# The second matrix product of a fused convolution and MLP kernel: 26 products of 4-row blocks in place of 5-row blocks, fewer VectorE taps, some sums as accumulating DMAs

## The chip, the cores and the metric

The kernel runs on one core of one Trainium2 chip. The metric is the device time of one execution in microseconds. Before the change it is 2314.07 us, the median of three runs (2314.03 to 2314.65).

## The reference

The input x has 8 sequences of 4096 tokens with 192 channels, in 32-bit floats. Eight heads of 24 channels each get a causal depthwise convolution of 7 taps, whose weights are a softmax over the taps. The result goes through a two-layer MLP with 2048 hidden units.

```python
w = softmax(weight, axis=-1)                  # (8 heads, 7 taps), 1e-9 in the divisor
out[b, s, h, g] = sum_k w[h, k] * x_pad[b, s + k, h, g]    # x padded by 6 zeros ahead
x = out.reshape(32768, 192)
h = x @ moe_w_in                              # (192, 2048)
g = h * (1 / (1 + exp(-1.702 * h)))
return g @ moe_w_out                          # (2048, 192), float32
```

The two weight matrices arrive as 64-bit values and are rounded on the chip.

## The kernel before

**Tiling.** The 32768 tokens are worked off in 32 steps, called `big`: 4 pairs of sequences times 8 chunks of 512 tokens, two chunks (one of each sequence) at a time. Step 0 is done apart (`first_step`, `second_first`), beside the rounding of the weights and the making of their sums; this first stage ends about 95 us into the run. Steps 1 to 31 are one loop. Tokens lie along the free axis, 256 (`T`) to a half, and channels and hidden units along the partitions.

**First product.** `hidden(big, v, ...)` runs twice a step, for v = 0 and v = 1, each for half of the hidden units. It is a product scheme with fewer multiplications than the plain one: 21 terms each, a list `TERMS` of sums of weights by sums of convolution blocks, and each term is a pair of two 64x512 matmuls on the two row halves of TensorE (L577). Terms gather in PSUM banks (`x`, `y`, `z`, `sums`), ScalarE copies some of them to SBUF (k15, k16, k18, k19, k20 in the tile `room`, L607), VectorE adds (L611) and ScalarE applies the Gelu with the sigmoid into the tile `g` (L598, L600).

**Second product.** `second(...)` makes out = g·w_out by a scheme of products of blocks: `g` has 16 rows of 128 hidden units, cut into 3 blocks of 5 rows and 1 row over. Sums of the blocks of `g` (VectorE, 128x1280, L649 to L693 in the second `hidden` and L893 to L930 in `second`) multiply forms, that is sums of blocks of w_out, made once in the first stage. A round is three matmuls of 128x256 on three column groups and a fourth, of a side product, on the column group left over (L867); there are 81 rounds. When a side product ends, ScalarE copies it out of PSUM (L881, 32x256), main products are copied by ScalarE (96x256) and joined by VectorE (L908 to L972), turned by VectorE (L819) and stored by DMA.

**The convolution for a later step.** While step big runs, step big + 2 is prepared. The channels are three blocks of 64. Each of two of them (c = 1, 2) is made by VectorE: seven instructions, one multiplication (L492) and six multiply-adds (L494). Block c = 0 is made by ScalarE, which multiplies (L501), and GpSimd, which adds (L505). GpSimd also makes the sums of convolution blocks (`sums_c`, L388 and L390). The blocks are then copied to the other half of the partitions by DMAs that SyncE issues (`cross`).

**What sets the order.** Every engine runs its instructions in the order of the program, which is written by hand: the scheduler is off (`manual_schedule`), and the framework adds the semaphores. VectorE's convolution work is a list (`todo`), taken from by `work(us)` at chosen places, as many items as the given number of microseconds holds by the costs noted beside them. The taps are another list (`ready`), taken from by `next_tap`: in `second`, one at every fourth round from 54 on (`LATE, EVERY = 54, 4`), and then all of the six additions that follow:

```python
for k in (*range(1, K), 0):
    yield "", 1.0, lambda k=k: tap_times(big, k)
for k in range(1, K):
    yield "", 0.0, lambda k=k: add_tap(big, k)
```

`need(label)` takes a list up to a label, `give` lets the copies of a step's blocks go, and `cross_when` holds them back until then.

Of the kernel before, what the change touches and what calls it, by code (L numbers as in the profile page):

```python
# [15 lines left out]
def kernel(  # L16
# [99 lines left out]
    NS, ND = 3, 5  # L116
    assert len(PAIRS) * 4 == NF == NS * ND + 1
    g = consts.tile([P, 2, NF, TOK], F32)


    ROW = {1: 2, 2: 0, 3: 1}
    COL = {1: (0, 0), 2: (0, 1), 3: (1, 1), 4: (1, 0)}

    def block(r, j):

        n, o = COL[j]
        i = ND * ROW[r]
        return g[:, n, i : i + ND, o * T : (o + 1) * T]

    def rest(j):  # L130
        n, o = COL[j]
        return g[:, n, NF - 1 :, o * T : (o + 1) * T]


# [6 lines left out]

    BLK = ND * T
    t_s = osbs[:, 0:BLK].rearrange("p (k t) -> p k t", k=ND)
    spare = consts.tile([P, 3, T], F32)
    t_a, t_8 = (
        flat_room[:, i * BLK : (i + 1) * BLK].rearrange("p (k t) -> p k t", k=ND) for i in range(2)
    )

    def kept(i):

        return flat_room[0 : NC * Q, 2 * BLK + i * T : 2 * BLK + (i + 1) * T]

    e0, e1, e2 = (spare[0 : NC * Q, i, :] for i in range(3))
    e3 = block(3, 3)[0 : NC * Q, 0, :]


# [59 lines left out]
    FORMS = 12  # L218
    F1, F3, F5, N7, F8, N9, F11, F13, N14, F15, F16, F19 = range(FORMS)
    w_form = consts.tile([P, FORMS, ND, HD], F32)  # L220

    def w_part(m, r):
        i = ND * ROW[r]
        return w_out_s[:, m - 1, i : i + ND, :]

    def form(i):
        return w_form[:, i, :, :]

    BEGIN_O = [
        (F1, (1, 1), 1), (F5, (1, 2), 1), (N14, (2, 1), 1), (F16, (1, 2), 1), (F13, (1, 2), -1),  # L230
        (F19, (2, 2), 1), (F15, (1, 1), 1), (F11, (1, 3), 1), (F3, (2, 3), 1),
    ]
    ADD_O = [(F1, (2, 1)), (F5, (1, 3)), (N14, (2, 3)), (F16, (2, 2)), (F13, N14), (F19, N14), (F15, F5)]
    BEGIN_2 = [(N9, F1, 1), (F8, F5, 1), (N7, F5, -1)]
    ADD_2 = [(N9, (2, 3)), (F8, (2, 2)), (N7, (2, 1)), (F11, N9), (F3, F8)]
    TURN_O = [(N14, N14, -1), (N9, N9, -1)]

# [6 lines left out]
    assert PIECE == CW * D and 3 * PIECE <= NB * T and 3 * PIECE <= 2 * NJ * XW and 3 * PIECE <= FORMS * ND * HD  # L244
    places = w_in_s[:, 4 * NC : NA, :].rearrange("p a f -> p (a f)")
    b12, b22 = (g[:, 1, i:, :].rearrange("p i t -> p (i t)") for i in (6, 2))
# [180 lines left out]
    def of_form(j):  # L427
        return w_part(*j) if isinstance(j, tuple) else form(j)

    def begin_forms(items):  # L430
        for dst, src, sign in items:
            if sign == 1:
                act.copy(form(dst), of_form(src))
            else:
                act.mul(form(dst), of_form(src), -1.0)

    def add_forms(items):
        for dst, src in items:
            nc.gpsimd.dma_start(out=form(dst), in_=of_form(src), accum_op=ALU.add)
# [35 lines left out]

    taps = [block(1, 3)[:, 0:2, :], block(1, 3)[:, 2:4, :], block(3, 1)[:, 3:5, :]]
    taps += [block(1, 4)[:, 0:2, :], block(1, 4)[:, 2:4, :], block(3, 3)[:, 3:5, :]]
    assert len(taps) == K - 1
    first_taps = [g[:, 0, k, :].rearrange("p (n t) -> p n t", n=2) for k in (2, 3, 6, 7, 10, 11)]

    def tap_home(big, k):
        return (first_taps if big < 3 else taps)[k - 1]
# [15 lines left out]
    def tap_times(big, k):  # L498

        dst = tap_home(big, k) if k else own(big)[:, 0:2, :]  # L500
        act.mul(dst, conv_src(big, 0, k), cw[:, 0, k : k + 1])  # L501

    def add_tap(big, k):
        dst = own(big)[:, 0:2, :]
        nc.gpsimd.tensor_add(dst, dst, tap_home(big, k))  # L505
# [22 lines left out]
    given = {True: 0, False: -1}  # L528

    def cross_when(early, *what):  # L530
        if given[early] < what[0] - 1:
            waiting[early].append(what)
        else:
            cross(*what)

    def give(early, big):
        given[early] = big
        for what in waiting[early]:
            cross(*what)
        waiting[early].clear()  # L540

    def prepare(big):
# [9 lines left out]
        yield from convs(2, 0) if big == 1 else convs(2, 1)  # L552
# [40 lines left out]
    def gelu(b, u, v, src):  # L593
        m, n = divmod(b, 2)
        i = 2 * (v * len(PAIRS) + PAIRS.index((m, u)))
        if isinstance(src, list):
            for h in range(2):
                act.activation(g[:, n, i + h, :], src[h], AF.Gelu_apprx_sigmoid)  # L598
        else:
            act.activation(g[:, n, i : i + 2, :], src, AF.Gelu_apprx_sigmoid)  # L600
# [17 lines left out]
    def hidden(big, v, x, z, y, sums, work, fetch, last=lambda: None):  # L618
# [5 lines left out]


# [3 lines left out]
        pe(sums, 12)  # L629
        copy2(k15, sums)  # L630
        pe(x, 5, 17)
# [3 lines left out]
        pe(sums, 0)  # L635
        copy2(k16, sums)
        last()
# [5 lines left out]
        if v or big == 1:  # L643
            work(3.2 if v else 1.6)
# [3 lines left out]
        if v:  # L648
            vec.tensor_add(t_s, block(2, 1), block(2, 4))  # L649
            vec.tensor_sub(block(2, 1), block(2, 1), block(3, 1))  # L650
        work(2.6 if v else 1.2)
# [3 lines left out]
        copy2(k18, x)  # L655
        pe(z, 11)
# [6 lines left out]
        work(1.1)  # L663
        gelu(B22, 1, v, k19)
        gelu(B22, 0, v, k15)
        pe(y, 8)
        pe(sums, 1, 9, first=True)
        pe(y, 15)
        if v and big == 1:
            turn_next()  # L670
        else:
            work(2.2 if big > 1 and not v else 1.1)
# [5 lines left out]
        if v:  # L678
            vec.tensor_sub(t_a, block(2, 3), block(3, 3))
# [5 lines left out]
        work(1.2)  # L685
# [3 lines left out]
        work(0.7)  # L689
        sum2(vec.tensor_add, k18, k18, sums)  # L690
        if v:
            vec.tensor_add(block(2, 3), block(2, 2), block(2, 3))
            vec.tensor_sub(t_8, t_s, block(3, 1))  # L693
# [5 lines left out]
    def second_first(fetch):  # L699
# [9 lines left out]

        ws = [w_out_s[:, m, :, :] for m in range(2)]  # L710
        gs = [g[:, n, :, :] for n in range(2)]
        a11, a12, a21, a22 = (four(t, pi) for t in ws for pi in first)
        b11, b12, b21, b22 = (four(t, pi) for pi in first for t in gs)
        t1, t2 = (place4(flat_room[:, i * nk * TOK : (i + 1) * nk * TOK]) for i in range(2))
        flat_spare = spare.rearrange("p i t -> p (i t)")
        w4 = nk * HD
        s1, s2 = (place4(flat_spare[:, i * w4 : (i + 1) * w4]) for i in range(2))
# [11 lines left out]
        def listed(w, t):  # L729
            return [(w[:, v, h, :], t[:, v, h, :]) for v in range(2) for h in range(2)]  # L730

        def plainly(m, n):
            return [p for pi in other for p in listed(four(ws[m], pi), four(gs[n], pi))]
# [35 lines left out]
        begin_forms(BEGIN_O)  # L769
        add_forms(ADD_O)  # L770
# [12 lines left out]
        begin_forms(BEGIN_2)  # L783
        add_forms(ADD_2)
# [47 lines left out]
    LATE, EVERY = 54, 4  # L832

    def second(big, bx, by, bs, vec_work, final, last):
# [4 lines left out]
        (m1, sa), (m2, m3), (sb, sc) = bx, bs, by  # L839
        s16, s21, s22, s2, s23, s12, v8, s14, s17, q13 = (kept(i) for i in range(10))  # L840
        s13, s4, s11 = (block(3, 1)[0:n3, i, :] for i in range(3))
        sc12, s1v, s24, u5 = e0, e1, e2, e3

        side, rounds_done = [], [0]

        def side_product(w, t, to, first=True, banks=(sa, sb, sc)):

            for c, bank in enumerate(banks):
                dst = bank[n3:, 0:T]
                for k in range(t.shape[1]):  # L850
                    last = k == t.shape[1] - 1
                    side.append((dst, w[:, k, chunk_cols(c)], t[:, k, :], first and k == 0, last and chunk(to, c)))

        one = lambda m: w_out_s[:, m - 1, NF - 1 :, :]
        side_product(w_part(2, 2), block(2, 4), s12)
        side_product(form(F16), block(2, 2), s16)
        if not last:
            side_product(one(2), rest(2), s22, first=False)
        side_product(form(F16), block(2, 1), s17)
        side_product(one(1), rest(1), s11, first=False)  # L860
        side_product(form(F1), block(1, 1), s1v)
        side_product(form(F1), block(1, 2), s4)
        if last:
            side_product(one(2), rest(2), s22, banks=(m3, m2, sb))
# [4 lines left out]
        def go(bank, h, w, t, first=True, left=None):  # L869

            dst = bank[0:n3, h * T : (h + 1) * T]
            steps = [(w[:, k, :], t[:, k, :]) for k in range(ND)]
            if left:
                steps.append((w_out_s[:, left[0] - 1, NF - 1, :], rest(left[1])[:, 0, :]))
            for k, (wk, tk) in enumerate(steps):
# [7 lines left out]
                if rounds_done[0] >= LATE and rounds_done[0] % EVERY == LATE % EVERY:  # L883
                    next_tap()
# [334 lines left out]
```

## Time and profile before

| | |
|---|---|
| median of three runs | 2314.07 us (2314.03 to 2314.65) |
| span of the profiled execution | 2312.2 us |
| that execution's own time | about 1.9 us over its span, by the median |
| TensorE busy | 2304.8 us, 100% |
| VectorE, ScalarE, GpSimd busy | 2005.1, 1376.9, 432.4 us |
| granted clock | 1.000 |
| DMA | 137.99 MB, mean 60 GB/s |

The span runs from the first instruction to the last. Busy times are those of instructions on the engine; the share is of the span. TensorE is named PE, its weight loads PEld, VectorE DVE, ScalarE ACT, GpSimd POOL and SyncE SP. A group of the profile is a line of the program, an engine, an operation, output and inputs by the program's names, shapes and a count; then the busy time of all and the mean duration of one in ns, then the idle time of the engine ahead of them and what ended most of it.

### The profile page before, as it was taken

What the parts mean: (1) busy time and instruction counts of PE and PEld (TensorE: products, weight loads), DVE (VectorE), ACT (ScalarE), POOL (GpSimd) and SP (SyncE); (2) the same over time, 40 slices, a digit from 0 to 9 for tenths busy, and PEclk for the clock granted to TensorE, in tenths of its full rate; (3) what the DMA queues carried; (4) which work ended last, traced back from release to release, by engine and by line L of the source; (5) the groups of instructions that cost most, each with busy time, mean ns of one, the idle gap of its engine ahead of it and who ended that gap; (6) DMA issues with size and microseconds to landing.
All of it is one profiled execution on the core that took longest, in us unless ns stands there. A gap on an engine that the chain in (4) does not pass through costs nothing.

```text
span 2312.2 us, 60320 instructions
## 1 busy us (share of the span) xinstructions
PE 2304.8 (100%) x25982; PEld 1217.8 (53%) x25982; DVE 2005.1 (87%) x2819; ACT 1376.9 (60%) x2554; POOL 432.4 (19%) x451
## 2 busy tenths in 40 slices
PE   9999999999999999999999999999999999999999
PEld 5355555555555555555555555555555555555556
DVE  8898889888898888898888988889888898888877
ACT  7555665566655556555566555665565655556644
POOL 0311222102221022211122211222102221022200
PEclk9999999999999999999999999999999999999999
DMA  8632322223221233112331132321223321231010
GB/s 185 121 67 60 70 52 47 56 57 70 65 48 43 57 70 70 42 43 58 70 70 43 44 69 57 70 53 45 57 57 70 68 45 43 57 70 45 17 43 16
DMA packets 199899, 137.99 MB, mean 60 GB/s; under 512 B 109008, under 2 KB 190544, under 8 KB 195664
## 3 DMA queue, kind: packets, MB, share of 16 engines
q1 hardware_dynamic: 197072, 130.98, 25.7%
q0 software_dynamic: 1728, 2.95, 0.8%
q8 instruction: 204, 3.34, 0.6%
q14 instruction: 63, 0.52, 0.1%
q10 hardware_dynamic: 832, 0.20, 0.0%
HBM read 53.15 MB, written 25.17 MB: 34 GB/s over the span
## 4 chain that ended last, share of the span: by engine, by line
PE 99%; ACT 0%; DVE 0%; DMA 0%; issue 0%; SPq 0%; DVEq 0%; ACTq 0%
PE slot L577 35%; PE slot L867 33%; PE sums L577 16%; PE sums L867 14%; PE slot L746 2%; DMA xin<-in_x_dram 0%; ACT conv_t L1029 0%; DVE xt L471 0%; DVE conv_t L494 0%; SPq L99 0%; ACT conv_t L354 0%; ACT conv_t L353 0%; DVE osbs L819 0%; ACT conv_t L523 0%; ACT conv_t L1025 0%
## 5 line engine op out<-in xcount | busy, mean ns | idle before, releaser
L577 PE MATMUL slot<-conv_t,w_in_s 64*128 64x512 f32 x3740 | 852.5, 590 | 0.3 <-DVE w_in_s L373 0.3
L867 PE MATMUL slot<-g,w_form 128*32 128x256 f32 x6700 | 772.5, 379 | 0.0
L577 PEld LDWEIGHTS slot<-conv_t,w_in_s 64*128 64x128 f32 x3740 | 369.0, 187 | 432.1 <-issue 386.9
L505 POOL TENSOR_TENSOR conv_t<-conv_t,g 128x512 f32<-128x512 f32 x180 | 244.8, 1360 | 1448.6 <-ACT conv_t L501 1436.8
L867 PEld LDWEIGHTS slot<-g,w_form 128*32 128x32 f32 x6700 | 399.6, 110 | 134.9 <-ACT g L598 23.5
L867 PE MATMUL sums<-g,w_form 128*32 128x256 f32 x3530 | 461.8, 379 | 0.0
L867 PE MATMUL slot<-g,w_out_s 128*32 128x256 f32 x4432 | 442.0, 379 | 0.0
L577 PE MATMUL sums<-conv_t,w_in_s 64*128 64x512 f32 x1660 | 405.4, 591 | 0.3 <-DVE w_in_s L373 0.3
L600 ACT ACTIVATE g<-room 128x1024 f32<-128x1024 f32 x310 | 324.5, 1073 | 90.9 <-DVE room L611 90.9
L494 DVE SCALAR_TENSOR_TENSOR conv_t<-xt,cw,conv_t 128x512 f32<-128x512 f32 (+1 forms) x390 | 309.3, 793 | 10.1 <-ACT conv_t L492 3.2
L867 PEld LDWEIGHTS slot<-g,w_out_s 128*32 128x32 f32 x4432 | 226.0, 110 | 97.5
L867 PEld LDWEIGHTS sums<-g,w_form 128*32 128x32 f32 x3530 | 233.3, 110 | 65.6
L607 ACT COPY room<-slot 128x512 f32<-128x512 f32 x434 | 231.5, 602 | 57.3 <-PE slot L577 57.3
L577 PEld LDWEIGHTS sums<-conv_t,w_in_s 64*128 64x128 f32 x1660 | 165.7, 187 | 189.1 <-issue 154.1
L598 ACT ACTIVATE g<-slot 128x512 f32<-128x512 f32 x334 | 179.7, 590 | 88.8 <-PE slot L577 88.8
L881 ACT COPY room<-slot 32x256 f32<-32x256 f32 x245 | 89.8, 367 | 205.8 <-PE slot L867 200.2
L867 PE MATMUL sums<-g,w_out_s 128*32 128x256 f32 x1706 | 205.3, 379 | 0.0
L867 PE MATMUL slot<-room,w_form 128*32 128x256 f32 x2340 | 182.1, 379 | 0.0
L611 DVE TENSOR_TENSOR room<-slot,room 128x512 f32<-128x512 f32 x248 | 156.1, 680 | 20.4 <-ACT room L607 20.4
L611 DVE TENSOR_TENSOR room<-room,sums 128x512 f32<-128x512 f32 x124 | 79.1, 679 | 70.2 <-PE sums L577 70.2
L611 DVE TENSOR_TENSOR room<-room,slot 128x512 f32<-128x512 f32 x124 | 79.1, 678 | 64.5 <-PE slot L577 64.5
L607 ACT COPY room<-sums 128x512 f32<-128x512 f32 x186 | 100.0, 591 | 58.8 <-PE sums L577 58.8
(212 smaller groups left out, 2665.5 us busy)
## 6 DMA issues: line engine op xcount, KB each, us to landing
xin<-in_x_dram SPq DMA_DIRECT2D x240, 180.0 KB, 4.1
conv_t<-conv_t SPq DMA_DIRECT2D x62, 512.0 KB, 6.2
out_dram<-osbs SPq DMA_DIRECT2D x186, 128.0 KB, 2.6
conv_t<-conv_t SPq DMA_DIRECT2D x62, 256.0 KB, 3.1
conv_t<-conv_t SPq DMA_DIRECT2D x62, 64.0 KB, 4.5
xin<-in_x_dram SPq DMA_DIRECT2D x16, 160.0 KB, 3.3
w_form<-w_out_s POOLq DMA_DIRECT2D x7, 240.0 KB, 4.1
osbs<-in_moe_w_out_dram SPq DMA_DIRECT2D x2, 768.0 KB, 8.3
```

The source lines that it names most:

```text
L494: vec.scalar_tensor_tensor(out=dst, in0=src, scalar=tap, in1=dst, op0=ALU.mult, op1=ALU.add)
L505: nc.gpsimd.tensor_add(dst, dst, tap_home(big, k))
L577: nc.tensor.matmul(slot[h], w_in_s[halves[h], a, v * P : (v + 1) * P], src, start=first, stop=True, skip_group_check=True,)
L598: act.activation(g[:, n, i + h, :], src[h], AF.Gelu_apprx_sigmoid)
L600: act.activation(g[:, n, i : i + 2, :], src, AF.Gelu_apprx_sigmoid)
L607: act.copy(bank(dst, h), bank(src, h))
L611: op(*(bank(t, h) for t in (dst, a, b)))
L746: nc.tensor.matmul(chunk(bank, c), w[:, chunk_cols(c)], t, start=first and i == 0, stop=not more and i == len(steps) - 1, skip_group_check ...
L867: nc.tensor.matmul(dst, w, t, start=first, stop=last, skip_group_check=True)
L881: act.copy(to, d)
```

## The change

- `second` becomes 26 products of blocks of 4 rows (4 blocks, no row over). There are 78 rounds, in the order of a list `PLAN` of items (main, side, go, sum, acc, seed, join, turn, store, tap, cross, final).
- `g` is laid out anew, as `[P, 4, 2, 2, 4, 256]`, and the Gelus write into it with a stride.
- There are 28 sums of blocks of g in a step: 22 on VectorE with 128x1024 (five in the second `hidden`, `EARLY_G`, seventeen in `PLAN`) and six as accumulating DMAs that GpSimd issues, of 512 KB each (one in `EARLY_G`).
- "Seeds" are copies, some negated, by ScalarE of a PSUM or SBUF value into PSUM or SBUF, ahead of a product that adds to it or of a join.
- Convolution block c = 2 leaves VectorE and becomes taps like c = 0, so there are 14 taps a step: seven in `PLAN`, from round 50 to 72, and seven in `hidden` with v = 0 (`taps_at`). Each tap now issues its multiplication and, but for the first of a block, GpSimd's addition right behind it.
- The copies to the other half of the partitions go in pieces of at most three blocks, at the `cross` items in `PLAN`.
- In `hidden` with v = 1 the calls of `work` go (but for step 1), and with v = 0 the first terms are in another order.
- The forms of w_out are made by 19 additions on GpSimd (128x384) and 6 negations on ScalarE, in place of copies on ScalarE and 12 accumulating DMAs.

```diff
-    NS, ND = 3, 5
+    NG = 4
...
-    g = consts.tile([P, 2, NF, TOK], F32)
+    g = consts.tile([P, NG, 2, 2, NG, T], F32)
...
+    SUMS_O = [
+        (8, 7, "+", 6), (9, 5, "+", 7), (10, 2, "+", 6), (11, 3, "-", 5), (12, 3, "-", 6), (13, 3, "+", 7),
...
-    def tap_times(big, k):
-
-        dst = tap_home(big, k) if k else own(big)[:, 0:2, :]
-        act.mul(dst, conv_src(big, 0, k), cw[:, 0, k : k + 1])
-
-    def add_tap(big, k):
-        dst = own(big)[:, 0:2, :]
-        nc.gpsimd.tensor_add(dst, dst, tap_home(big, k))
+    def tap(big, c, k):
+
+        dst = own(big)[:, 2 * c : 2 * c + 2, :]
+        home = tap_home(big, c, k) if k else dst
+        act.mul(home, conv_src(big, c, k), cw[:, c, k : k + 1])
+        if k:
+            nc.gpsimd.tensor_add(dst, dst, home)
...
+    def cross_now(early, big, b0, b1):
+        if early or big == 1:
+            cross(big, b0, b1)
+        else:
+            pieces.extend((big, b, min(b + 3, b1)) for b in range(b0, b1, 3))
...
-        yield from convs(2, 0) if big == 1 else convs(2, 1)
+        yield from convs(2, 0) if big == 1 else convs(1)
...
-        for k in (*range(1, K), 0):
-            yield "", 1.0, lambda k=k: tap_times(big, k)
-        for k in range(1, K):
-            yield "", 0.0, lambda k=k: add_tap(big, k)
+        for c in (0, 2):
+            for k in range(K):
+                yield "", 1.0, lambda c=c, k=k: tap(big, c, k)
...
+        else:
+            pe(x, 5)
+            pe(sums, 12)
+            copy2(k15, sums)
+            pe(x, 17)
+            taps_at(1)
         gelu(B11, 0, v, x)
         if not v:
             pe(z, 7, first=True)
         pe(sums, 0)
+        taps_at(1)
         copy2(k16, sums)
+        taps_at(2)
         last()
...
-        work(2.6 if v else 1.2)
+        early(1)
+        if not v or big == 1:
+            work(1.2)
         pe(sums, 13)
         copy2(k19, sums)
         pe(x, 2)
         copy2(k18, x)
+        taps_at(2)
...
+    EARLY_G = [
+        [(6, 6, "-", 10)], [(1, 7, "-", 6), (1, 1, "-", 11)], [(0, 5, "+", 6), (8, 0, "acc")],
+        [(2, 9, "-", 0)],
+    ]
+    PLAN = [
...
+        ("tap",), ("go", 2), ("main", 21, 7, "p2", 0), ("go", 1), ("sum", 6, 14, "+", 6), ("go", 1), ("tap",),
+        ("side", 7, 20, "k1"), ("go", 2), ("sum", 6, 6, "-", 17), ("main", 10, 14, "p0", 0), ("go", 2),
+        ("tap",), ("seed", "k5", "p2", 1), ("cross",), ("join", "k10", "k10", "+", "k8"), ("go", 2),
+        ("join", "p2", "p4", "+", "k3"), ("main", 8, 8, "p1", 0, 0, 2), ("go", 1),
+        ("join", "k8", "k9", "+", "k5"), ("tap",), ("go", 1), ("join", "k8", "k7", "-", "k8"),
+        ("main", 4, 6, "p4", 0), ("go", 1), ("turn", 1, 0, 1, "k10"), ("go", 1),
+        ("join", "k3", "p1", "+", "k6"), ("go", 1), ("tap",), ("join", "k3", "p0", "-", "k3"), ("go", 1),
+        ("join", "k6", "k0", "-", "p0"), ("side", 8, 5, "k0"), ("main", 15, 12, "p2", 0), ("go", 2),
+        ("join", "k7", "k4", "-", "p4"), ("go", 1), ("tap",), ("join", "k7", "k7", "+", "k3"), ("go", 1),
+        ("join", "k2", "k2", "-", "k1"), ("main", 12, 18, "p3", 0), ("go", 1), ("turn", 0, 0, 0, "k7"),
+        ("go", 1), ("join", "k6", "k6", "+", "p4"), ("tap",), ("go", 1), ("turn", 1, 1, 1, "k2"), ("go", 1),
+        ("turn", 1, 0, 0, "k6"), ("store", 0, 0), ("main", 24, 19, "p5", 0), ("go", 2), ("final",),
...
+    ]
+
+    def sum_g(dst, a, op, b=None):
+
+        if op == "acc":
+            nc.gpsimd.dma_start(out=spot(dst), in_=spot(a), accum_op=ALU.add)
+        else:
+            add_up(spot, dst, a, op, b)
...
+        for item in PLAN:
+            ops[item[0]](*item[1:])
...
-        second(big, x, y, sums, work, lambda: copy2(sums, z) if more else None, not more)
+        second(big, x, y, sums, lambda: copy2(sums, z) if more else None, not more)
```

In `PLAN`, "go n" issues n rounds, "main f s to" starts the product of form f by block or sum s into the PSUM half-bank to (p0 to p5, two to a bank), "side" does the same for the fourth column group, and "join", "seed", "turn" name half-banks or SBUF values of 96x256 (k0 to k11). Spots 0 to 4 of the sums are scratch, those from 5 on are the sixteen blocks of `g` itself.

More of the change, by code (lines that the diff above doesn't have):

```diff
@@ L474, in transpose_x, with tap_home @@
         )
[L476 to L482, printed above, removed]
+    taps = [spot(i)[:, k : k + 2, :] for i in TAP_SPOTS for k in (0, 2)]
+    first_taps = [row(0, k) for k in (2, 3, 6, 7)]
+    def tap_home(big, c, k):
+        return (first_taps if big < 3 and c == 0 else taps)[(3 * c + k - 1) % len(taps)]
     def conv_src(big, c, k, ns=slice(0, 2)):
@@ L677, in hidden @@
         gelu(B21, 1, v, x)
[L678 to L679 removed]
+        early(3)
         fetch()
@@ new lines, with second, value, product @@
+    SIDE_HALF = (0, 0, 1, 0, 1, 0, 1)
+    def second(big, bx, by, bs, final, last):
+        n3 = NC * Q
+        mains, sides = (bs[0], bx[0], by[0]), (bx[1], bs[1], by[1])
+        side, count = [], [0]
+        now = {}
+        stored = {0: 0, 1: 0}
+        def value(name):
+            i = int(name[1:])
+            return mains[i // 2][0:n3, i % 2 * T : (i % 2 + 1) * T] if name[0] == "p" else kept(i)
+        def product(f, s, k0=0, k1=NG):
+            return [(form(FORM_OF[f])[:, k, :], spot(s)[:, k, :]) for k in range(k0, k1)]
@@ L866, in one_matmul, with begin_side @@
         def one_matmul(dst, w, t, first, last):
             nc.tensor.matmul(dst, w, t, start=first, stop=last, skip_group_check=True)
[L869 to L875, printed above, removed]
+        def begin_side(f, s, to, *ks):
+            steps = product(f, s, *ks)
+            for c in range(NC):
+                turns, i = divmod(count[0], NC)
+                h = SIDE_HALF[turns]
+                count[0] += 1
+                dst = sides[i][n3:, h * T : (h + 1) * T]
+                for k, (w, t) in enumerate(steps):
+                    end = k == len(steps) - 1
+                    side.append((dst, w[:, chunk_cols(c)], t, k == 0 and h == 0, end and chunk(value(to), c)))
@@ L972, in second, with seed, out_turn @@
-        add(s22, s22, q13 if last else s4)
-        done(2, 2, s22)
-        if last:
-            store(big, 0, 1, (nc.scalar, nc.sync, nc.scalar))
-        else:
-            store(big, 0)
-        assert not side
+        def seed(dst, src, sign):
+            if sign == 1:
+                act.copy(value(dst), value(src))
+            else:
+                act.mul(value(dst), value(src), -1.0)
+        def out_turn(m, n, o, src):
+            turn(m, n, blocks(value(src)), slice(o * T // Q, (o + 1) * T // Q))
@@ new lines, in out_store @@
+        def out_store(n, o):
+            if last:
+                queues = (nc.sync, nc.scalar) if o else (nc.scalar, nc.sync)
+                store(big, n, o, queues + queues[0:1])
+                return
+            stored[n] += 1
+            if stored[n] == 2:
+                store(big, n)
+        ops = dict(
+            sum=sum_g, acc=lambda d, a: sum_g(d, a, "acc"), main=begin_main, side=begin_side, go=go, seed=seed,
+            join=lambda d, a, op, b: add_up(value, d, a, op, b), turn=out_turn, store=out_store,
+            tap=next_tap, cross=cross_piece, final=final,
+        )
@@ L980 @@
+        for item in PLAN:
+            ops[item[0]](*item[1:])
+        assert not side and not now["steps"] and count[0] == NC * len(SIDE_HALF)
+        while pieces:
+            cross_piece()
     todo, ready = [], []
```

279 lines of the change are left out of this document (93 added, 186 removed), and 24 rows, old and new, of tables (PLAN, SUMS_O).

## The prediction

> **What bounds the kernel now.** First the totals of the page, its clock row and the chain of waits:
>
> ```profile
> PE 2304.8 (100%) x25982; PEld 1217.8 (53%) x25982; DVE 2005.1 (87%) x2819; ACT 1376.9 (60%) x2554; POOL 432.4 (19%) x451
> ...
> PEclk9999999999999999999999999999999999999999
> ...
> PE 99%; ACT 0%; DVE 0%; DMA 0%; issue 0%; SPq 0%; DVEq 0%; ACTq 0%
> PE slot L577 35%; PE slot L867 33%; PE sums L577 16%; PE sums L867 14%; PE slot L746 2%; DMA xin<-in_x_dram 0%; ACT conv_t L1029 0%; DVE xt L471 0%; DVE conv_t L494 0%; SPq L99 0%; ACT conv_t L354 0%; ACT conv_t L353 0%; DVE osbs L819 0%; ACT conv_t L523 0%; ACT conv_t L1025 0%
> ```
>
> The reader is to see that TensorE never stops: whatever the others do is hidden, and the clock never falls. So a round less is worth its full time, and any wait that appears is paid in full. Then the timeline of TensorE: one second product (L867) begins at 1059.48 and the next first product (L577) at 1094.58, so 81 rounds take 35.10 us, **0.4333 us each**; a big step is 36.25 + 35.10 us. The groups by shape price what moves:
>
> ```profile
> L494 DVE SCALAR_TENSOR_TENSOR conv_t<-xt,cw,conv_t 128x512 f32<-128x512 f32 x378 | 303.5, 803 | 9.9 <-ACT conv_t L492 3.2
> L505 POOL TENSOR_TENSOR conv_t<-conv_t,g 128x512 f32<-128x512 f32 x180 | 244.8, 1360 | 1448.6 <-ACT conv_t L501 1436.8
> L501 ACT ACTIVATE g<-xt,cw 128x512 f32<-128x512 f32 x180 | 126.5, 719 | 2.3
> ...
> L881 ACT COPY room<-slot 32x256 f32<-32x256 f32 x245 | 89.8, 367 | 205.8 <-PE slot L867 200.2
> ...
> L893 DVE TENSOR_TENSOR g<-g 128x1280 f32<-128x1280 f32 x31 | 46.0, 1484 | 0.0
> ...
> L959 DVE TENSOR_TENSOR room<-room 96x256 f32<-96x256 f32 x30 | 38.9, 1297 | 0.0
> L972 DVE TENSOR_TENSOR room<-room,g 96x256 f32<-96x256 f32 x30 | 29.6, 987 | 0.0
> L966 DVE TENSOR_TENSOR spare<-spare,g 96x256 f32<-96x256 f32 x30 | 28.3, 944 | 3.5 <-DVE spare L964 0.5
> L911 DVE TENSOR_TENSOR room<-room 96x256 f32<-96x256 f32 x31 | 12.9, 415 | 0.0
> L964 DVE TENSOR_TENSOR spare<-spare,slot 96x256 f32<-96x256 f32 x31 | 12.6, 406 | 0.7 <-PE slot L867 0.7
> ```
>
> L959, L966 and L972 are joins of the same shape as L911, yet two to three times as long. The timelines of GpSimd and VectorE at the end of one second product say why:
>
> ```profile
> 1093.75 8.53 POOL L505 TENSOR_TENSOR conv_t<-conv_t,g 128x512 f32<-128x512 f32 x6 [49.47 <-ACT conv_t L501]
> ```
>
> ```profile
> 1093.98 1.33 DVE L959 TENSOR_TENSOR room<-room 96x256 f32<-96x256 f32 x1
> 1095.24 0.40 DVE L964 TENSOR_TENSOR spare<-spare,slot 96x256 f32<-96x256 f32 x1
> 1095.75 0.97 DVE L966 TENSOR_TENSOR spare<-spare,g 96x256 f32<-96x256 f32 x1
> ```
>
> A join of two SBUF values that meets one of GpSimd's adds waits for it; L964, with one input in PSUM, doesn't. This costs nothing now, because those joins feed only the store.
>
> **Part 1, the rounds.** 81 − 78 = 3 rounds × 0.4333 us × 31 second products = **−40.3 us**, all on the path. First product unchanged.
>
> **Part 2, VectorE.** 16 sums of 128x1280 at 1.48 go; 22 of 128x1024 come, about 1.22 each (between 0.415 for 256 columns at L911 and 1.484 for 1280 lie 0.27 per 256 columns): 26.8 − 23.7 = +3.1 us. Conv block 2 goes: 0.48 + 6 × 0.80 = −5.3. Net −2 of some 62 busy in 71.35: VectorE doesn't become the bound.
>
> **Part 3, ScalarE.** +7 taps × 0.72 and 6 copies × 0.37 = +7.3 on about 43 of 70 us: room on average, but the order is fixed, so place by place below.
>
> **Part 4, GpSimd and the DMAs.** +6 adds × 1.36 and 6 issues × 0.86 (one issue alone, in the first stage): 14 to 27 us of 70. Each accumulating DMA moves 512 KB and is read 8.4 us after its issue or later, by the order. Bounds: 3.3 us (240 KB alone) and 11.3 (the median 5.3 of the five 240 KB accumulations, times 512/240). Packets of 1920 B took 0.168 us: 273 of them over 16 engines are 2.9 us, and some 2 to landing. I take 5 to 8: no stall. SP gets the half-swaps in pieces of at most three blocks, 6 more per step inside the product; the plain 512 KB one landed in 6.2, and nothing reads a piece before the next first product: 0. On GpSimd's own queue the issues stand between sums and adds; the last one, of spot 14 onto 18, is ahead of the first add, so a late source there would hold up all the adds behind it.
>
> **Part 5, waits that appear.** With t = 0 at the start of a second product, round r begins at 0.4333 r.
> (a) Round 62 writes over p4; TensorE waits for the join p2 = p4 + k3, and this for ScalarE's seed k5←p2, which is queued behind the side copy of round 58 and tap 2. Copy until 25.31, tap (0.719, less overlap) 25.70, seed 26.80, join 27.24, against 26.87 due: **0.42** with the 0.05 of a semaphore. If tap 2 fell between the copies as now (1.04 idle before L881), 0.
> (b) Round 74 starts p5, in the bank of p4; it waits for k6 = k6 + p4, on VectorE behind ten joins and two transposes that begin when (a) ends. Joins at a pitch of 0.34 (0.45 where the one before feeds it) would end at about 31.2, against 32.49 due: no wait. But taps 1 to 6 now come at rounds 50 to 69, so five adds run just here. Three joins meet one: k8 until 28.01, k8' until 29.42, k7' until 32.18, 2.1 us lost (L959, L966 and L972 lose 0.88, 0.53 and 0.57; three are 2.0). k6 ends at 33.28: **0.80**. The bounds are 0 and, if the sixth add, queued at 32.10, also goes ahead of join k2, 34.3: 1.85. I take 0.80: join k2 is ready at about 32.11, since joins overlap by 0.07 (0.415 long at a pitch of 0.34), and nearly ties with the add; a tap 0.02 later decides for VectorE. Hence the weight of B below.
> (c) Next hidden, v = 0: the eighth term overwrites the bank that ScalarE copies to k16, and two taps are now ahead of it: it ends at 6.49 against 6.11: **0.40**. The bound below is 0.22, with taps at the pitch of 0.63 that they have one behind another (two × 0.09 less); above, at the 0.73 before a PSUM copy, 0.42. The swapped first terms (x5 ahead of the sums) cost nothing: the sums' bank, copied last, gets one term, 0.86, more room.
> (d) In v = 1 the remaining adds delay VectorE's conv operations (L494 took 1.45 instead of 0.80 at 1099.71) by 1.3; k20 comes at 15.4, gelus B11, B21 and copy y follow 1.1 late, with 0.5 to 0.8 of slack: **0.35** (0 to 0.6).
> Sum 1.97 us per step, in the 29 steps that have taps: 57.1.
>
> [...]
>
> **Part 6, the first stage.** Nineteen weight sums on GpSimd (128x384, about 1.0 by L505's 1.36 for 512) replace copies and 12 DMAs; they are needed at about 127 us and end by 104 to 121: 0, within ±3.
>
> Sum: −40.3 + 57.1 = +16.8, on the profiled execution's 2312.2 span with about 1.9 around it (the median of three is 2314.07): **2331**.
>
> **The rivals.** A, above: 2331, 35%.
> B, the sixth add goes first: (b) is 1.85, the step 3.02, 87.6 − 40.3: **2361**, 23%. For it: in the first stage two L494 took 2.45 and four L505 6.48 from 97.06 on, in turn, so an add that stands there does get its turn; against it: the tie needs every tap on time, and (a) moves VectorE, not ScalarE, later.
> C, the other side: the joins' waits don't reach TensorE. Place: the order of taps around rounds 50 to 72; below 1.39 us per step (40.3/29) the kernel is faster. With (a) and (c) alone, 0.82 × 29 = 23.8: **2298**; without them 2274. For it: joins with a PSUM input (L964) escape, and a seed taken a little earlier removes (a) and moves all of (b). Against it: 8.53 us of adds must lie somewhere, and six more do. 21%.
> D, half of it: (b) meets one add fewer or (a) is absorbed, 1.0 to 1.5 per step: 2303 to **2318**, 14%.
> E, an accumulating DMA lands late: 8.4 against the upper bound 11.3; 1 us beyond slack in 31 steps on top of A is **2362**, 7%. Against it: the 2.9 us by packets.
>
> **How the numbers follow.** 2331 is the likeliest case. The range takes B, E and half of C in: 2290 to 2364; A's own range is 2322 to 2340 ((a) to (d) ±0.3 per step). 0.2%, 4.6 us, is about what a measurement here can tell from no change. Faster: C and half of D, 28%; same: most of the rest of D, 6%; slower: the remainder, 66%.
>
> **What would show it.** L928 (the new product line) busy 3/81 lower; TensorE idle before it at round 62, released by VectorE, 0.4; at round 74 by VectorE, 0.8 (B: 1.8); in the first product by ScalarE's copies 0.4 and 0.35. Joins between taps of 1 us and more. [...]

## The result, and the profile after

The changed kernel takes **2388.72 us** (2388.54 to 2390.05), against 2314.1: 1.0323 times as long, 95% interval 1.0308 to 1.0338. That is 74.6 us slower, where the prediction had 17, and outside its range (2290 to 2364). The span is 2387.0 us, 74.8 more than before.

The totals of the page, its clock row and the chain of waits, which answer to those shown of before:

```profile
PE 2302.0 (96%) x25238; PEld 1347.5 (56%) x25238; DVE 2070.8 (87%) x2794; ACT 1545.0 (65%) x2942; POOL 892.7 (37%) x824
...
PEclk9999999999999999999999999999999999999999
...
PE 83%; DVE 9%; ACT 2%; issue 0%; ACTq 0%
PE slot L578 32%; PE slot L928 26%; PE sums L578 15%; PE sums L928 10%; DVE room L389 5%; DVE room L387 3%; DVE osbs L846 1%; ACT g L494 1%; DVE slot L387 1%; ACT room L957 0%; ACT room L953 0%; ACT w_out_s L433 0%; ACTq L953 0%; ACT room L615 0%; ACT w_form L433 0%
```

TensorE now stops: the chain has VectorE's joins in it (L387 and L389, the helpers that add and subtract). TensorE's waits, in total, times and longest, say where:

```profile
PE sums L928 <- DVE room L387: 26.4, 15, 1.8
PE slot L928 <- DVE room L387: 23.5, 14, 1.8
PE slot L578 <- issue: 8.8, 1, 8.8
PE slot L578 <- ACT room L615: 7.3, 1, 7.3
...
PE sums L928 <- DVE slot L387: 4.4, 15, 0.3
PE slot L928 <- DVE slot L387: 4.1, 14, 0.3
```

Two waits come once a step (29 times, on two tiles in turn, as the PSUM slots change places), and the two longest only once, in the first stage. The waits of the first product are not in this list: each is short (0.45 at the start of v = 1), or holds one row group of TensorE while the other works (0.29 at the eighth term). By the starts of the products on TensorE's timeline the account is:

| stretch | before | after | in all |
|---|---|---|---|
| up to step 1's first product | 95.49 | 106.92 | +11.4 |
| step 1's first products | 36.39 | 47.65 | +11.3 |
| second product, 30 of them | 35.10 | 36.27 (28 steps), 35.19 (one), 33.81 | +31.8 |
| first products, the other 30 | 36.25, the last 35.39 | 36.99, the last 35.39 | +21.5 |
| last second product | 35.29 | 34.00 | −1.3 |

Without waits the second product is 33.81, 78 rounds of 0.433, so it loses 2.47 us in nearly every step. Here is one such second product, which began at 1033.88. VectorE's joins from round 62 to the one that round 74 waits for:

```profile
1060.66 0.43 DVE L387 TENSOR_TENSOR slot<-sums,room 96x256 f32<-96x256 f32 x1 [2.38 <-ACT room L957]
1061.00 0.93 DVE L387 TENSOR_TENSOR room<-room 96x256 f32<-96x256 f32 x1
1061.96 1.39 DVE L389 TENSOR_TENSOR room<-room 96x256 f32<-96x256 f32 x1
...
1064.06 0.42 DVE L389 TENSOR_TENSOR room<-slot,room 96x256 f32<-96x256 f32 x1
...
1065.17 0.99 DVE L387 TENSOR_TENSOR room<-room 96x256 f32<-96x256 f32 x1
1066.08 1.49 DVE L389 TENSOR_TENSOR room<-room 96x256 f32<-96x256 f32 x1
1067.49 0.43 DVE L846 STREAM_TRANSPOSE osbs<-room 96x256 f32<-96x256 f32 x1
1067.86 0.37 DVE L387 TENSOR_TENSOR room<-room,sums 96x256 f32<-96x256 f32 x1
```

GpSimd's additions beside them:

```profile
1060.38 6.92 POOL L496 TENSOR_TENSOR conv_t<-conv_t,g 128x512 f32<-128x512 f32 x5 [0.44 <-ACT g L494]
```

The four joins whose inputs are both in SBUF take 0.93 to 1.49 us instead of 0.42; those with an input in PSUM, as the one at 1064.06, keep 0.37 to 0.43. The last line is k6 = k6 + p4: it begins at 33.98 into the product, and round 74 starts at 34.41, 1.9 late. The first line is the join of round 62, for which VectorE waited 2.38 on ScalarE's seed (L957); TensorE starts that round 0.48 late.

The first stage has its own lines. VectorE's sums of w_in, the first three before the change (first line) and the first six after it, beside the taps of step 2:

```profile
85.79 1.22 DVE L390 TENSOR_TENSOR w_in_s<-w_in_s 128x256 f32<-128x256 f32 x3
...
95.65 4.23 DVE L389 TENSOR_TENSOR w_in_s<-w_in_s 128x256 f32<-128x256 f32 x3
99.80 4.29 DVE L387 TENSOR_TENSOR w_in_s<-w_in_s 128x256 f32<-128x256 f32 x3
```

All six take 1.4 to 1.5 us each instead of 0.4. And they began at 95.65, before the change at 85.79: GpSimd's first fifteen sums of forms, from 59.13 to 84.31, had held VectorE up by that time already. The same three of VectorE's convolution operations before and after, and four of those sums:

```profile
68.91 2.32 DVE L494 SCALAR_TENSOR_TENSOR conv_t<-xt,cw,conv_t 128x512 f32<-128x512 f32 x3
...
75.15 4.31 DVE L486 SCALAR_TENSOR_TENSOR conv_t<-xt,cw,conv_t 128x512 f32<-128x512 f32 x3
...
76.05 5.43 POOL L387 TENSOR_TENSOR w_form<-w_out_s,w_form 128x384 f32<-128x384 f32 x4
```

TensorE started step 1's first product at 106.92, 9.4 us after the matmul before it. And ScalarE's queue, 30 us after that start:

```profile
136.54 0.52 ACT L433 ACTIVATE w_out_s<-w_out_s 128x384 f32<-128x384 f32 x1 [6.86 <-POOL w_out_s L389]
```

This negation of a form waits for GpSimd's last sum, and the copies that TensorE needs are queued behind it: a gap of 7.94 us.

### The profile page after: what moved, and what is told of

It is laid out like the page before. It is cut to its first block, busy times and chain, and to the rows that moved or that the text cites. A ratio compares the mean times of both kernels' runs of the same rounds, so it can differ in the third digit from the quotient of the medians.

```text
span 2387.0 us, 60716 instructions
## 1 busy us (share of the span) xinstructions
PE 2302.0 (96%) x25238; PEld 1347.5 (56%) x25238; DVE 2070.8 (87%) x2794; ACT 1545.0 (65%) x2942; POOL 892.7 (37%) x824
## 4 chain that ended last, share of the span: by engine, by line
PE 83%; DVE 9%; ACT 2%; issue 0%; ACTq 0%
PE slot L578 32%; PE slot L928 26%; PE sums L578 15%; PE sums L928 10%; DVE room L389 5%; DVE room L387 3%; DVE osbs L846 1%; ACT g L494 1%; DVE slot L387 1%; ACT room L957 0%; ACT room L953 0%; ACT w_out_s L433 0%; ACTq L953 0%; ACT room L615 0%; ACT w_form L433 0%
## 5 line engine op out<-in xcount | busy, mean ns | idle before, releaser
L578 PE MATMUL slot<-conv_t,w_in_s 64*128 64x512 f32 x3740 | 957.0, 595 | 16.4 <-issue 8.8
L496 POOL TENSOR_TENSOR conv_t<-conv_t,g 128x512 f32<-128x512 f32 x360 | 489.5, 1360 | 563.6 <-ACT g L494 548.7
L578 PEld LDWEIGHTS slot<-conv_t,w_in_s 64*128 64x128 f32 x3740 | 499.1, 187 | 351.3 <-issue 230.0
L578 PE MATMUL sums<-conv_t,w_in_s 64*128 64x512 f32 x1660 | 496.4, 594 | 0.3 <-DVE w_in_s L372 0.3
L389 DVE TENSOR_TENSOR g<-g 128x1024 f32<-128x1024 f32 x372 | 448.7, 1234 | 3.9 <-ACT g L604 0.7
L928 PE MATMUL sums<-g,w_form 128*32 128x256 f32 x2648 | 369.5, 379 | 0.0
L928 PE MATMUL slot<-g,w_out_s 128*32 128x256 f32 x4080 | 319.5, 380 | 27.7 <-DVE room L387 23.5
L904 POOL DMA_DIRECT2D g<-g x124 | 106.6, 860 | 525.7 <-DVE g L389 353.6
L494 ACT ACTIVATE g<-xt,cw 128x512 f32<-128x512 f32 x360 | 257.9, 743 | 2.2
L486 DVE SCALAR_TENSOR_TENSOR conv_t<-xt,cw,conv_t 128x512 f32<-128x512 f32 (+1 forms) x210 | 223.6, 1065 | 7.8 <-ACT conv_t L484 3.0
```

Of the source, the lines that this page charges most:

```text
L389: eng.tensor_sub(v(dst), v(a), v(b))
L486: vec.scalar_tensor_tensor(out=dst, in0=src, scalar=tap, in1=dst, op0=ALU.mult, op1=ALU.add)
L494: act.mul(home, conv_src(big, c, k), cw[:, c, k : k + 1])
L496: nc.gpsimd.tensor_add(dst, dst, home)
L578: nc.tensor.matmul(slot[h], w_in_s[halves[h], a, v * P : (v + 1) * P], src, start=first, stop=True, skip_group_check=True,)
L904: nc.gpsimd.dma_start(out=spot(dst), in_=spot(a), accum_op=ALU.add)
```

## The experiments

The theory after the result: GpSimd's additions make VectorE's instructions with two SBUF inputs wait (joins of 0.93 to 1.49 us in place of 0.42), and TensorE's wait in round 74 follows from that; the rest is order, ScalarE's taps in two places and two queues in the first stage. Rivals are given with each.

**GpSimd's additions in the second product.**

```diff
-        if k:
+        if k and not quiet[0]:
             nc.gpsimd.tensor_add(dst, dst, home)
```

`quiet[0]` is true while `PLAN` takes a tap.

> Leaves out part of the computation: GpSimd's additions of the taps that are issued inside the second product (convolution block 0), so those convolution values are wrong; ScalarE's multiplications all stay. Changed kernel: 2388.7. Theory (VectorE's joins wait for these additions, and TensorE waits for the joins in round 74): the wait of about 2.0 us in round 74 goes in 29 steps, 0.45 in round 62 stays, so 2388.7 - 58 = 2331. Rival (ScalarE's taps and seeds make the joins late, whoever adds): round 74 still waits 1.5 to 2, time 2375 to 2389.

Measured: 2333.19 us. The same joins, and the one that frees the bank (last line), in this run, in a product that began at 1011.25:

```profile
1038.37 0.41 DVE L387 TENSOR_TENSOR room<-room 96x256 f32<-96x256 f32 x1
1038.81 0.42 DVE L389 TENSOR_TENSOR room<-room 96x256 f32<-96x256 f32 x1
...
1041.04 0.42 DVE L387 TENSOR_TENSOR room<-room 96x256 f32<-96x256 f32 x1
1041.38 0.41 DVE L389 TENSOR_TENSOR room<-room 96x256 f32<-96x256 f32 x1
...
1042.08 0.38 DVE L387 TENSOR_TENSOR room<-room,sums 96x256 f32<-96x256 f32 x1
```

All four are back at 0.41 to 0.42, the bank is free at 30.8 + 0.4, and the product takes 34.31: the wait of 1.9 is gone, that of round 62 stays and costs 0.50. ScalarE is busy 17.99 us in this product, as in the one shown above. The theory holds: the additions are the cause.

**GpSimd's additions in the first product.** The same edit, with `quiet[0]` true in `taps_at` from step 2 on.

> Leaves out part of the computation: GpSimd's additions of the taps that are issued inside the first product (convolution block 2), from step 2 on; ScalarE's multiplications stay. Theory: the wait of about 0.4 us at the start of v = 1 is from VectorE's convolution operations waiting for these additions, and goes (29 x 0.4 = 12): 2376; the 0.29 at the eighth term is from ScalarE's taps ahead of the copy and stays. Rival (both waits are ScalarE's): 2386 to 2389.

Measured: 2376.70 us, and a first product of 36.54, 0.45 less. What stays is 0.29 at the eighth term, on one of the two row groups of TensorE only. So the two waits have two causes, as expected.

**The join that frees the bank, earlier.**

```diff
-        ("join", "k7", "k4", "-", "p4"), ("go", 1), ("tap",), ("join", "k7", "k7", "+", "k3"), ("go", 1),
+        ("join", "k7", "k4", "-", "p4"), ("join", "k6", "k6", "+", "p4"), ("go", 1), ("tap",), ("join", "k7", "k7", "+", "k3"), ("go", 1),
...
-        ("go", 1), ("join", "k6", "k6", "+", "p4"), ("tap",), ("go", 1), ("turn", 1, 1, 1, "k2"), ("go", 1),
+        ("go", 1), ("tap",), ("go", 1), ("turn", 1, 1, 1, "k2"), ("go", 1),
```

> One join, k6 = k6 + p4, which frees the bank that round 74 writes, is moved ahead of three joins and a transpose to right behind k7 = k4 - p4; nothing else. Theory (round 74 waits only for the queue ahead of this join on VectorE, which GpSimd's additions lengthen): the join ends about 2.6 us earlier, before round 74 is due, the wait of 2.0 goes: 2388.7 - 58 = 2331, with VectorE's joins at 1 us and more as before. Rival (the lateness is passed on: the joins at the end of the second product, or the banks of the next first product, are what TensorE waits for instead): 2365 to 2389.

Measured: 2344.0 us. The second product is 34.31, as without the additions: with all additions there, order alone takes the wait of round 74 away. But the first product grows from 36.99 to 37.35: ScalarE's copy to k15 now waits for p5 + k5, the last join to read that room.

```profile
1052.01 1.07 ACT L615 COPY room<-slot 128x512 f32<-128x512 f32 x2 [1.84 <-DVE room L387]
```

So a fifth of the gain (0.36 of 1.97) was passed on; both the theory and its rival have a part.

**The forms by DMA, as before the change.**

```diff
-            add_up(form, dst, a, op, b, eng=nc.gpsimd)
+            if op == "+":
+                act.copy(form(dst), form(a))
+            else:
+                act.mul(form(dst), form(b), -1.0)
+            nc.gpsimd.dma_start(out=form(dst), in_=form(b if op == "+" else a), accum_op=ALU.add)
```

> The 19 sums of forms of w_out are made as before the change, by a ScalarE copy and an accumulating DMA that GpSimd issues, not by GpSimd's additions. Theory (in the first stage these additions hold VectorE up by 9.9 us, and the last four of them hold ScalarE and so TensorE up by 7.9): the two waits of 9.4 and 7.9 us fall to 0 to 3 each, and the slow clock behind them goes: 2388.7 - 22.7 to - 14: 2366 to 2375. Rival (the first stage is late by the taps of step 2 and the chain of sums itself, by whatever engine): 2383 to 2395.

Measured: 2383.86 us, a miss: it lies in the rival's range. VectorE is back in time (w_in's sums begin at 86.08), and the first product starts at 95.78 and not 106.92. But two waits took the place: a gap of 3.5 us at 102.34, because the taps of step 2 still slow w_in's last sums (until 100.4, against 94.0), and one of 10.2 us at 132.79, behind this line of ScalarE:

```profile
131.33 0.52 ACT L437 ACTIVATE w_out_s<-w_out_s 128x384 f32<-128x384 f32 x1 [7.62 <-DMA w_out_s<-w_out_s]
```

The four late sums are queued on GpSimd behind step 2's additions and sums of convolution blocks, whoever adds; the negations wait for them, and the copies for the negations. So who adds the forms mattered for the first wait alone.

**Late negations.** The six negations are issued just before step 1's second product:

```diff
         need("forms")
+        while turns:
+            turns.pop()()
```

> The changed kernel with one move: the six negations of forms on ScalarE stand at the end of step 1's first products, not ahead of the copies of v = 1; the sums on GpSimd stay. Theory (ScalarE's queue stood for 6.9 us at a negation that waits for GpSimd's last sum, with the copies for TensorE behind it): the wait of 7.9 us goes with the slow clock behind it, 2388.7 - 9 = 2380, the other wait of 9.4 us stays. Rival (the same wait appears at the second product's first round): 2387 to 2389.

Measured: 2382.01 us, 6.7 of the 9 expected. Step 1's second product begins at 145.54 instead of 154.57, but 1.1 us come back in that product (37.48 instead of 36.36), 0.3 in a later one, and the one step with 35.19 took 36.27 here. The rival is out; the theory took the whole wait for gain.

**Three moves in the second product.** Besides the early join:

```diff
-        ("tap",), ("seed", "k5", "p2", 1), ("cross",), ("join", "k10", "k10", "+", "k8"), ("go", 2),
+        ("seed", "k5", "p2", 1), ("tap",), ("cross",), ("join", "k10", "k10", "+", "k8"), ("go", 2),
...
-        ("join", "k1", "p3", "-", "k3"), ("go", 1), ("turn", 0, 0, 1, "k1"), ("store", 0, 1), ("go", 1),
-        ("join", "k2", "p2", "-", "k4"), ("turn", 0, 1, 1, "k2"), ("store", 1, 1),
-        ("join", "k1", "p5", "+", "k5"), ("turn", 0, 1, 0, "k1"), ("join", "k8", "k8", "+", "k0"),
+        ("join", "k2", "p2", "-", "k4"), ("join", "k1", "p3", "-", "k3"), ("go", 2),
+        ("join", "k10", "p5", "+", "k5"), ("turn", 0, 0, 1, "k1"), ("store", 0, 1), ("turn", 0, 1, 1, "k2"),
```

> The early join of the third experiment, and two more moves in the second product: seed k5 goes ahead of the tap that stood before it, and the last joins (k2 = p2 - k4, k1 = p3 - k3, p5 + k5) go ahead of their transposes. Theory: the wait of 0.45 in round 62 was the tap's (13 us in 29 steps), and the 0.36 that the early join passed on to the next first product was the copy to k15 waiting for p5 + k5 (10 us): 2344.0 - 23 = 2321, a second product of 33.86, a first of 36.99. Rival (the seed gains nothing, since the additions of GpSimd that it delays by 0.37 hold the later joins instead): the second product stays at 34.2 and more, 2332 to 2340.

Measured: 2320.55 us. Every second product takes 33.81, without a wait, and the first 36.99 again.

**The first product too.**

```diff
-        taps_at(1)
         copy2(k16, sums)
...
         gelu(B22, 0, v, k15)
-        taps_at(1)
+        taps_at(2)
...
-        elif not v:
-            work(2.2 if big > 1 else 1.1)
+        elif not v and big == 1:
+            work(1.1)
         sum2(vec.tensor_add, k20, k20, sums)
         sum2(vec.tensor_sub, k16, y, k16)
+        if not v and big > 1:
+            work(2.2)
```

> The fifth, and in the first product with v = 0 one tap of the two ahead of the copy to k16 goes behind the gelus of B22, and VectorE's convolution operations there go behind the two sums for k20 and k16. Theory: the 0.29 at the eighth term (one tap) and the 0.4 at the start of v = 1 (the convolution operations that wait for GpSimd, ahead of those sums) both go: a first product of 36.25 to 36.35, 2321 - 20 = 2301. Rival (the tap moved behind the gelus, or the additions that now come later, make the copies at the start of v = 1 late): a first product of 36.6 to 37, 2311 to 2321.

Measured: 2365.34 us, worse than the one before and than the rival. The waits at the eighth term and at the start of v = 1 are gone, but a new one of 1.6 comes later, at 24.0 into the first product. VectorE at that place:

```profile
1077.06 4.69 DVE L486 SCALAR_TENSOR_TENSOR conv_t<-xt,cw,conv_t 128x512 f32<-128x512 f32 x4
1081.84 2.10 DVE L465 STREAM_TRANSPOSE xt<-xin 128x576 f32<-128x576 f32 x3
1083.86 1.25 DVE L619 TENSOR_TENSOR room<-room,slot 128x512 f32<-128x512 f32 x2
```

The sum for k18 (last line) stands behind the four operations that were moved back, slowed by GpSimd from 3.1 to 4.7, and the three transposes.

**The first stage too.** The same with forms by DMA, late negations and step 2's block 0 as before the change, with six homes and its additions last:

```diff
-    first_taps = [row(0, k) for k in (2, 3, 6, 7)]
+    first_taps = [row(0, k) for k in (2, 3, 6, 7, 10, 11)]
...
+        if big == 2:
+            for k in (*range(1, K), 0):
+                yield "", 1.0, lambda k=k: times(k)
+            for k in range(1, K):
+                yield "", 0.0, lambda k=k: add(k)
```

> The sixth, and the first stage: forms by ScalarE copies and accumulating DMAs as before the change, the six negations of forms at the end of step 1's first products instead of ahead of the copies of v = 1, and the taps of step 2's block 0 as before the change (all multiplications, then all additions). Theory (all that was lost in the first stage is those three): the second product of step 1 begins at 132 to 135 and not at 154.6: 2301 - 21 = 2280. Rival (the first stage has another limit, such as the new layout or the weight sums): it begins at 142 and later, 2288 and more.

Measured: 2340.86 us, 24.5 less than the sixth. Step 1's second product begins at 132.88, 1.0 after that of the kernel before: the three causes together hold all of the first stage's loss but one microsecond. The third, the taps of step 2, was not changed alone; that they slow VectorE's sums is read from the trace of the fourth. The total is 61 us above its forecast, as the sixth was 64 above its own.

**All but the convolution's order.** The seventh without the `work(2.2)` move.

> The seventh without the move of VectorE's convolution operations in the first product. Theory: what the sixth and seventh lost (a first product of 38.54) is VectorE's sum for k18, which stood behind four convolution operations and three transposes; with the operations back in their place the first product is 36.99 - 0.29 = 36.70, the second 33.81, step 2 begins where it did: 2340.9 - 29 x 1.84 = 2288. Rival (the tap that was moved behind the gelus is what made it late): 2325 to 2341.

Measured: **2289.56 us**, 0.9893 of before (0.9878 to 0.9908), a first product of 36.69 and a second of 33.81. So it was the operations' order that spoilt the sixth, not the tap that moved.

**All of it, with the transposes later.**

```diff
-        if not v and big > 1:
-            turn_next()
         pe(sums, 3, 19)
...
         sum2(vec.tensor_add, k18, k18, sums)
+        if not v and big > 1:
+            turn_next()
```

> The seventh, and the three transposes of x at the end of v = 0 go behind the sum for k18. Theory: the sum comes 2.06 us earlier, the wait of 1.6 goes, and the first product is 36.25 to 36.45: 2340.9 - 29 x 2.2 = 2277. Rival (the transposes make VectorE late in v = 1 instead): 36.7 and more, 2288 to 2330.

Measured: 2339.14 us, above even the rival's range: a first product of 38.48. The wait moved on, from the sum for k18 to the first sum of v = 1 (slot L636), 1.2 to 1.3 us in each of 28 steps, which now has the transposes (2.08) ahead of it:

```profile
PE slot L595 <- DVE slot L636: 34.8, 28, 1.3
```

**Without the accumulating DMAs.** The ninth, and in `sum_g`:

```diff
-            nc.gpsimd.dma_start(out=spot(dst), in_=spot(a), accum_op=ALU.add)
+            add_up(spot, dst, dst, "+", a)
```

> The ninth with the six accumulating DMAs of a step as sums on VectorE (128x1024). Theory (the DMAs cost TensorE nothing, and VectorE hasn't the room): six sums of 1.23 are 7.4 us more per step on VectorE, of which about 2.5 to 5 are not covered: 2288 + 29 x 2.5 to 5, so 2360 to 2433. Rival (VectorE's gaps hold them, the DMAs buy nothing): 2285 to 2300.

Measured: 2392.67 us, 103 above the ninth. The second product grows to 37.19, and VectorE is busy 37.0 of them. So these DMAs save 3.4 us a step, and in the changed kernel no wait of TensorE was released by one.

**One convolution operation each way.** The ninth, and:

```diff
-            work(1.2)
+            work(1.9 if big > 1 else 1.2)
...
-            work(2.2 if big > 1 else 1.1)
+            work(1.4 if big > 1 else 1.1)
```

> The ninth, with one of VectorE's convolution operations moved forward into its idle 1.1 us ahead of the sums for k19, and one moved back behind the sums for k20 and k16, so that two and not four stand ahead of those. Theory (the 0.42 left at the start of v = 1 is the gelu of k20, late behind four operations that take 4.87): these take 1.6 to 2.4 less, the wait goes, a first product of 36.25 to 36.35: 2289.6 - 29 x 0.4 = 2278. Rival (the operation moved back makes the sum for k18 late, as in the sixth): 36.7 to 37.5, 2290 to 2313.

Measured: **2276.45 us**, 0.9836 of before (0.9819 to 0.9852). Three operations (3.57 us), not four (4.87), now stand ahead of the sum for k20 (the expectation had counted two), and that is enough. The page of this kernel, its totals and the chain's shares:

```profile
PE 2265.6 (100%) x25238; PEld 1196.6 (53%) x25238; DVE 2019.2 (89%) x2794; ACT 1559.1 (69%) x2961; POOL 949.7 (42%) x824
...
PE 98%; ACT 1%; DVE 1%; DMA 1%; issue 0%; POOL 0%; SPq 0%; DVEq 0%; ACTq 0%
```

From step 2 on TensorE doesn't stop, and a step is 36.25 + 33.81. The products of the change are all kept; only the order differs, and in the first stage who adds the forms.

## Why the prediction was wrong

Of the 57.7 us between the forecast and the measured time, 35 are in the second product, 33 of them from the choice in (b), and 22.7 in the first stage, Part 6. These two steps failed.

- **Part 1, the rounds: right.** 33.81 without waits, 1.29 below 35.10; the last kernel is 37.7 below the one before, against 40.3; of the rest 1.0 is in the first stage, 0.8 in step 1's second product (34.65) and 0.9 behind TensorE's last matmul.
- **Part 2: the price right, the net not.** The sums of 128x1024 take 1.21 to 1.23 in the mean (1.22 taken). But VectorE is busy 64.2 us a step, 62.5 before, where the prediction had 2 less: what it waits for GpSimd counts as busy. In the first experiment, without these additions, it is busy 29.8 in a second product and not 32.6.
- **Part 3: right in kind.** ScalarE is busy 48.4 us a step, 5.7 more than before; 7.3 was predicted.
- **Part 4: right.** The accumulating DMAs land in 4.5 to 5.8 us by the medians of their groups (5 to 8 taken), single ones in up to 9.2, and none released a wait of TensorE; rival E is out. Neither did a half-swap in pieces.
- **Part 5 (a): right.** 0.42 predicted; round 62 starts 0.48 late, which lengthens the product by 0.50, and the seed ahead of the tap takes it away.
- **(b): the mechanism right, the choice between its two ends wrong.** The two ends were 0.80 and 1.85; round 74 starts 0.86 late in one step and 1.94 late in 28. The prediction took 0.80 because join k2 was to come out ahead of the sixth addition in a near-tie. In the 28 steps the addition starts 0.04 to 0.06 us ahead of the join. In the step shown above it starts at 32.14 into the product (32.10 predicted), the join at 32.20 (32.11), and waits. In the one step that went the other way, VectorE:

```profile
2165.10 0.41 DVE L389 TENSOR_TENSOR room<-room 96x256 f32<-96x256 f32 x1
```

and GpSimd:

```profile
2165.09 1.55 POOL L496 TENSOR_TENSOR conv_t<-conv_t,g 128x512 f32<-128x512 f32 x1 [0.20 <-ACT g L494]
```

Here the addition, started 0.05 later in the product because ScalarE's tap came 0.04 later, takes 1.55 and the join 0.41. So rival B was the case, and the other side of the near-tie costs 1.1 us in 28 steps, some 30 us. The working could not settle this tie: its two times are off by 0.04 and 0.09 us and lay 0.01 apart, so to name A rather than B was a guess. In the 28 steps the addition, which starts first, takes 1.26 to 1.27 us and the join 1.48 to 1.51; in the other the two start within 0.01 us, too close for this trace to tell their order.
- **(c) and (d): the sum right, the split not.** 0.40 + 0.35 predicted; 0.29 (on one row group, within the bounds given) and 0.45, 0.74 together.
- The sum of a step was thus 1.97 by A and 3.02 by B; measured is 3.21.
- **Part 6, the first stage: put at nothing, and wrong.** "0, within ±3", and it is +22.7. The first fifteen sums ended at 84.3 and the last four at 136.5, not by 104 to 121. The prediction compared the end of GpSimd's sums with their need and asked nothing more. It had priced in (b) what an addition on GpSimd does to VectorE, but didn't apply this to the fifteen sums (VectorE 9.9 us late) and to the taps of step 2. And it overlooked that the negations are queued on ScalarE ahead of the copies for TensorE, so that a late sum stops the engine (6.86 us at 136.54) before the sum's own reader is due. B with this loss would have been 2361 + 22.7 = 2384, 5 us from the measured time. Without this loss the kernel would have taken about 2366 (2388.7 − 22.7), and the range ended at 2364: with (b) as it came out, there was no room for anything in Part 6.

## What to carry to other kernels

An instruction given to an idle engine isn't free if, as here, it makes another engine's instructions wait (joins of 0.42 us that take 0.93 to 1.49): price it at every place where it comes to stand, the set-up stage included. For a wait, ask who is queued behind the one that waits, not only when the result is needed. Where the bound engine is full, the order of a few joins decides the sign: with the same products, sums and taps this change was 3.2% slower, and with a dozen items moved, and the forms added as before, 1.6% faster than the kernel before; and work moved back from one wait made the next one twice (the sixth and tenth).

## What the runs showed of the hardware that was not expected

In the changed kernel the granted clock fell from 1.00 to 0.50 in the two long waits of the first stage and stayed there behind them. In and behind the gap of 9.4 us, whose last matmul before ended at 98.13, and behind that of 7.9, by windows (the first line names the columns; PEclk is the granted clock):

```profile
core 0: us, PE busy (x) PEld busy (x) DVE busy (x) ACT busy (x) POOL busy (x), PEclk, DMA share, GB/s
98.15:100.15 2.00, 0.00 (x0) 0.00 (x0) 1.97 (x3) 1.92 (x4) 1.84 (x3) 1.00 0.37 94
100.25:102.25 2.00, 0.00 (x0) 0.00 (x0) 2.00 (x2) 1.30 (x3) 1.92 (x2) 0.50 0.00 0
106.90:108.90 2.00, 1.98 (x6) 1.21 (x8) 1.90 (x6) 0.00 (x0) 0.00 (x0) 0.50 0.36 77
108.90:110.90 2.00, 2.00 (x9) 1.05 (x7) 1.97 (x5) 0.26 (x1) 0.00 (x0) 0.62 0.00 0
110.90:112.90 2.00, 2.00 (x12) 1.30 (x10) 2.00 (x4) 2.00 (x5) 0.00 (x0) 1.00 0.00 0
138.00:140.00 2.00, 2.00 (x5) 1.78 (x7) 1.04 (x2) 1.42 (x3) 0.00 (x0) 0.50 0.00 0
```

It fell about 2.0 us into the first gap, at 100.17, and 3.7 into the second, at 134.31 (last matmul before ended at 130.65). After the matmuls started again it was 0.50 for another 3.1 to 3.5 us, so each of these waits cost 1.6 to 1.8 us more than itself, by an estimate (half of that time); the gap of 7.94 with both makes the 11.3 of step 1's first products in the table above. The waits of 1.9 us in the 28 steps (1.8 of them idle) left it at 1.00. With the forms by DMA it was low behind a gap of 3.5 us, 2.9 of them idle (0.66 from 102.3 to 104.3, 0.50 from 104.3 to 106.3).

The two matmuls of a term, on two row groups, parted: in the changed kernel's first product that begins at 1070.15, one group waits 0.30 at the eighth term and keeps that lag to the end of v = 0, while the other goes on in time. Four matmuls of one term took 1.32 us there from the first start to the last end (at 1081.41), and 1.02 in the kernel before (at 1034.49). In the second experiment the wait of 0.29 at the eighth term is all that is left above 36.25.
